# Loading w2 and the last query weights over two groups of a backward pass, and making rows in small tasks

## The chip, the cores and the metric

The kernel runs on one core of one Trainium2 chip. The metric is the device time of one execution in microseconds. The core has a matrix engine (PE), two engines for elementwise work (DVE and ACT), GpSimd (POOL) and SyncE (SP), and its transfers run on 16 DMA engines that SP, ACT and POOL issue to.

## The reference

A decoding step of one token is run through four layers, attention, MLP, attention, MLP, all with shared weights, and then everything is differentiated. One attention layer and one MLP layer:

```
q = layernorm(x) @ wq                      # 1024 -> 32 heads x 128
scores = q . k_cache * 128**-0.5           # 4 KV heads, 65536 positions
o = softmax(scores) . v_cache              # 8 query heads per KV head
x = x + o @ wo
h = relu(layernorm(x) @ w1 + b1) ** 2      # 1024 -> 3584
x = x + h @ w2 + b2
```

The outputs are the final x (out_0) and the gradients of x, k_cache, v_cache, wq, wo, w1, b1, w2 and b2. Everything is bfloat16. The two caches are 67 MB each and are read in every pass; their gradients are written, 67 MB each. The gradient of a weight is a sum of two outer products, one per layer that uses it.

## The kernel before, in words

There are four passes over K and V, each over four groups (the KV heads). A pass is a software pipeline of 256 items, 64 per group (`IPG`); an item is 8 blocks of 128 positions. The first two passes are the forward attention layers, the third (`attn_bwd3`) is the backward pass of the second attention layer, and the fourth (`attn_bwd4`) is that of the first and writes the gradients of K and V for both layers at once. A K or V slab of 1 MB holds 4 items.

**Third pass.** Item i transposes a V block group (`vT`, L799, copied out of PSUM at L152 or L155 by `evac`, which chooses ACT or DVE by a running count of their load), multiplies it (`vS`, L820) two items later, and uses K (`k8`, L842) eleven items after `vT`. `Stream.fetch` issues a slab on SP's queue (L249) at its first use in program order; SP runs ahead of the engines until the slot that it wants is free. The slots are a ring, least recently used first: areas 0 to 4 and 6 to 13 at the start of this pass, 13 slots of 1 MB. `ring.remove` takes a slot out.

**Background work.** `at(bg, i, fn)` hangs a task on item i. `in_order` ties the first instruction of a task on each engine behind the one before it there; otherwise the framework's scheduler orders instructions.

In the third pass the background does three things. `og3.later` makes dots of Wo rows for the next group. `qg3.early` makes dots of Wq rows with the finished groups' query gradients (`dot_va`, L380 on DVE and L381 on ACT): groups 0 and 1 together with eight loads of 512 KB through the ring, and group 2 with eight loads of 256 KB on ACT's queue (L749) into `area[5]`. And w2, needed twice: as it is for the forward MLP of layer 4 (`mv_slab`, L358, giving out_0), and transposed for the backward MLP of layer 2 (`pg2`, L1133). Its 28 blocks of 128 rows pass through a buffer of four rows in `area[6]`:

```
    i0 = IPG * (G - 1) + 10
    for k in range(8):
        at(bg, i0 - 14 + 8 * max(0, k - 1), lambda k=k: ring.remove(area[6 + k]))
    for kc in range(FC):
        at(bg, i0 + 2 * kc - 6, lambda kc=kc: w2_fetch(kc))
        at(bg, i0 + 2 * kc, lambda kc=kc: w2_block(kc))
    at(bg, i0 + 2 * FC, w2_done)
```

`w2_fetch` issues on SP's queue (L1099); `w2_block` multiplies, transposes (L1108) and copies the transposed block into areas 7 to 13. `w2_done` stores out_0 (L292, on SP's queue).

**Between the passes.** `qg3.last` loads the Wq columns of the last group after the pass and makes their dots by `row_dots` (L414 to L434), ending in L744. Then follow the layer norm's backward step, `pg2`, the dots of W1 (`RowDots`, with W1 loaded through the ring), another layer norm step, the first Wo dots and the start of the fourth pass. In the fourth pass the last group's Wq product is made another way: `qg1.transposed` has transposed the weights before, and `last_transposed` (L769 to L775) multiplies them with the column.

**Fourth pass.** Beside `vT`, `vS` and `k8` (with the K and V gradients made at L960 and stored at L967 and L968 by POOL's queue), a list of tasks (`gw_tasks`) is spread evenly over items 72 to 253. `rows_into` puts two columns into rows of `long_rows` or `short_rows` (casts at L976, products with the identity at L981 into `ps_gg`, copies on DVE at L982), up to 32 column blocks in one task; `outer2` makes pieces of the weight gradients (L1006) and stores them (L1010). `ps_gg` has two buffers, shared by the K and V gradients and all these tasks. `g_setup` prepares a group's operands (L867 to L885), at the first `vS` of the group.

Of the kernel before, what the change touches and what calls it, by code (L numbers as in the profile page):

```python
# [14 lines left out]
P = 128  # L15
# [3 lines left out]
def kernel(  # L19
# [830 lines left out]
    def attn_bwd4(La, Lb, oga, ogb, order, eTa, eTb, dqT, bg, group_done, streams):  # L850
# [4 lines left out]
        XT = Turn([blocks(small, i) for i in (3, 4)])  # L855
        XS = Turn([part(small, i, 1024) for i in (5, 6)])
        GGS = Turn([part(area[5], i, 512) for i in range(2)])
        ndt4 = part(small, 14, 512)[0:64, :].rearrange("p (s r) -> p s r", r=R2)
        ST = Turn([pair[6], pair[8], pair[10]])
        DOB = vec.tile([P, G, 4, R2], BF, name="DOB")  # L860
        nc.vector.memset(DOB[:], 0.0)
# [2 lines left out]

        def g_setup(g):
            sl = slice(g * R, (g + 1) * R)
            nc.vector.tensor_copy(out=DOB[:, g, 0, 0:R], in_=oga.dOT[:, sl])  # L867
            nc.vector.tensor_copy(out=DOB[:, g, 0, R:R2], in_=ogb.dOT[:, sl])
            CCf = tmp.tile([P, R4], F32, name="CCf")
            nc.vector.scalar_tensor_tensor(out=CCf[:, 0:R], in0=La["qT"][:, sl], scalar=SCALE, in1=La["rZ"][:, sl], op0=ALU.mult, op1=ALU.mult)  # L870
            nc.vector.scalar_tensor_tensor(out=CCf[:, R:R2], in0=Lb["qT"][:, sl], scalar=SCALE, in1=Lb["rZ"][:, sl], op0=ALU.mult, op1=ALU.mult)
            nc.vector.tensor_tensor(out=CCf[:, R2:3 * R], in0=oga.dOT[:, sl], in1=La["rZ"][:, sl], op=ALU.mult)
            nc.vector.tensor_tensor(out=CCf[:, 3 * R:R4], in0=ogb.dOT[:, sl], in1=Lb["rZ"][:, sl], op=ALU.mult)
            CC4 = tmp.tile([P, 4, R4], BF, name="CC4")
            nc.vector.tensor_copy(out=CC4[:, :, :], in_=CCf[:, :].unsqueeze(1).to_broadcast([P, 4, R4]))
            pt = ps_mv([P, P], BF)
            nc.tensor.transpose(pt[:, :], CC4[:].rearrange("p a b -> p (a b)"), ident_b[:, :])
            T4 = tmp.tile([P, P], F32, name="T4")
            nc.vector.tensor_copy(out=T4[:], in_=pt[:, :])
            GG = GGS.next().rearrange("p (c t d) -> p c t d", c=2, t=2)  # L880
            for c2 in range(2):
                for t in range(2):
                    nc.vector.tensor_scalar(out=GG[:, c2, t, :], in0=T4[:], scalar1=M4x[:, 2 * c2 + t:2 * c2 + t + 1], scalar2=None, op0=ALU.mult)
            nc.vector.tensor_copy(out=ndt4[:, :, 0:R], in_=oga.nd2[:, sl].unsqueeze(1).to_broadcast([64, UB4, R]))
            nc.vector.tensor_copy(out=ndt4[:, :, R:R2], in_=ogb.nd2[:, sl].unsqueeze(1).to_broadcast([64, UB4, R]))  # L885
            state[("G", g)] = GG
# [10 lines left out]

        def vS(idx):
            g, c8 = kit[idx]
            if c8 == 0:  # L900
                g_setup(g)
            vt = state.pop(("vt", idx))
            for i in range(8):
                c = c8 + i
                slot = c % UB4
                if slot == 0:
                    state["ps_dp"] = ps_sc([P, UB4, R2])
                    nc.tensor.matmul(state["ps_dp"][:, :, :].rearrange("p c r -> p (c r)"), lhsT=sel2[:, :],
                                     rhs=ndt4[:, :, :].rearrange("o c r -> o (c r)"), start=True, stop=False)
                ps_dp = state["ps_dp"]  # L910
                last = slot == UB4 - 1
                w = min(4, UB4 - slot)
                nc.tensor.matmul(ps_dp[:, slot:slot + w, :].rearrange("p a b -> p (a b)"), lhsT=vt[:, i, :],  # L913
                                 rhs=DOB[:, g, 0:w, :].rearrange("p a b -> p (a b)"), start=False, stop=last)
                if last:
                    c0 = c - slot
                    X = XS.next().rearrange("p (s r) -> p s r", r=R4)
                    ea = eTa[g][:, :, c0:c0 + UB4].rearrange("p h c -> p c h")
                    eb = eTb[g][:, :, c0:c0 + UB4].rearrange("p h c -> p c h")
                    nc.vector.tensor_tensor(out=X[:, :, 0:R], in0=ps_dp[:, :, 0:R], in1=ea, op=ALU.mult)  # L920
                    nc.vector.tensor_tensor(out=X[:, :, R:R2], in0=ps_dp[:, :, R:R2], in1=eb, op=ALU.mult)  # L921
                    nc.gpsimd.tensor_copy(out=X[:, :, R2:3 * R], in_=ea)
                    nc.gpsimd.tensor_copy(out=X[:, :, 3 * R:R4], in_=eb)
                    add_load(dve=2 * (0.07 + UB4 * R * 0.0021))
                    nblk = UB4 // 4
                    pt2 = ps_tr()
                    for bi in range(nblk):
                        nc.tensor.transpose(pt2[:, bi, :], X[:, 4 * bi:4 * bi + 4, :].rearrange("p a b -> p (a b)"), ident_b[:, :])  # L928
                    xt = XT.next()
                    evac(xt[:, 0:nblk, :], pt2[:, 0:nblk, :])  # L930
                    state[(g, c0 // UB4)] = (X, xt)

        def k8(idx):
# [32 lines left out]
            if j0 + 8 == J:  # L966
                nc.gpsimd.dma_start(out=GKv[g][b], in_=st[:, 0, :, :])  # L967
                nc.gpsimd.dma_start(out=GVv[g][b], in_=st[:, 1, :, :])  # L968

        pipeline(n, [(vT, 0), (vS, TLEAD), (k8, TLEAD + UB4 // 8 + 1)], bg)  # L970


    def rows_into(rows, cols, nj):
        cc = tmp.tile([P, 32, 2], BF, name="r2_cc")
        for l in range(2):
            nc.vector.tensor_copy(out=cc[:, 0:nj, l], in_=cols[l])  # L976
        for j0 in range(0, nj, 4):
            jn = min(4, nj - j0)
            pt = ps_gg()
            for jj in range(jn):  # L980
                nc.tensor.matmul(pt[0:2, jj * P:(jj + 1) * P], lhsT=cc[:, j0 + jj, :], rhs=ident_b[:, :], start=True, stop=True)  # L981
            nc.vector.tensor_copy(out=rows[0:2, j0 * P:(j0 + jn) * P], in_=pt[0:2, 0:jn * P])  # L982

    def outer2(stages, out_dram, a_rows, K, b_rows, c0, N):

# [101 lines left out]
    for j, g in enumerate(ORD3[1:]):  # L1087
        og3.later(vbc_small, g, bg, IPG * j + 12, 1)
    qg3 = QueryGrad(dqT3, "B3")
    qg3.early(ORD3[:2], bg, IPG * 2 + 14, 2.6, area[5])  # L1090
    qg3.early(ORD3[2:3], bg, IPG * 3 + 14, 3, area[5], Turn([part(area[5], i, 1024) for i in (1, 2, 3)]), 6)


    w2rows = Turn([part(area[6], i, 1024) for i in range(4)])
    w2T, w2_here = {}, {}

    def w2_fetch(kc):
        w2_here[kc] = w2rows.next()
        nc.sync.dma_start(out=w2_here[kc], in_=B_w2[kc * P:(kc + 1) * P, :])  # L1099

    def w2_block(kc):
        rows = w2_here.pop(kc)
        if kc == 0:
            L4["pf"] = ps_bg([P, DC])
        mv_slab(L4["pf"], rows, kc, FC, D, L4["gb"][:, kc:kc + 1])
        pt = ps_tr()
        for i in range(DC):
            nc.tensor.transpose(pt[:, i, :], part(rows, i, P), ident_b[:, :])  # L1108
        w2T[kc] = blocks(area[7 + kc // 4], kc % 4)
        evac(w2T[kc], pt[:, :, :])  # L1110

    def w2_done():
        mlp_close(L4, L4["pf"][:, :])
        col_to_dram(L4["xo"], D, out_0.rearrange("a b d -> (a b d)"))
    i0 = IPG * (G - 1) + 10
    for k in range(8):
        at(bg, i0 - 14 + 8 * max(0, k - 1), lambda k=k: ring.remove(area[6 + k]))
    for kc in range(FC):
        at(bg, i0 + 2 * kc - 6, lambda kc=kc: w2_fetch(kc))
        at(bg, i0 + 2 * kc, lambda kc=kc: w2_block(kc))  # L1120
    at(bg, i0 + 2 * FC, w2_done)
    attn_bwd3(L3, og3, ORD3, eT3, dqT3, bg)


    dn3 = qg3.last(ORD3[-1], area[5])
    dxn3 = ln_bwd(dn3[:], L3["n"], L3["rstd"])
    dx2 = add_cols(dx3[:], dxn3[:], "dx2")
    dx2b = tmp.tile([P, DC], BF, name="dx2b")
# [41 lines left out]
        nc.gpsimd.memset(long_rows, 0.0)  # L1170
        nc.gpsimd.memset(short_rows, 0.0)

    def rows_of(rows, cols, nj):
        return lambda: rows_into(rows, cols, nj)

    def gwq_tasks(gs, fresh=True):
        gs = sorted(gs)
        a, b = gs[0] * R, (gs[-1] + 1) * R
        if fresh:
            yield rows_of(short_rows, [L3["n"][:], L1["n"][:]], DC)  # L1180
        yield rows_of(long_rows, [dqT3[:, a:b], dqT1[:, a:b]], b - a)
        yield from outer2(stages, out_4, short_rows, D, long_rows, gs[0] * GD, len(gs) * GD)

    def gw_tasks():
        yield rows_of(short_rows, [gx[:], dx2[:]], DC)
        yield rows_of(long_rows, [L4["g"][:], L2["g"][:]], FC)
        yield from outer2(stages, out_8, long_rows, F, short_rows, 0, D)
        yield rows_of(short_rows, [L4["n"][:], L2["n"][:]], DC)
        yield rows_of(long_rows, [dh4[:], dh2[:]], FC)
        yield from outer2(stages, out_6, short_rows, D, long_rows, 0, F)  # L1190
        yield from gwq_tasks(ORD4[0:2])
        yield rows_of(short_rows, [dx3[:], dx1[:]], DC)
        yield rows_of(long_rows, [L3["oT"][:], L1["oT"][:]], HQ)
        yield from outer2(stages, out_5, long_rows, QD, short_rows, 0, D)
        yield from gwq_tasks(ORD4[2:3])

# [6 lines left out]
    qg1 = QueryGrad(dqT1, "B1")  # L1203
    done = [IPG * (j + 1) + LAG4 + 1 for j in range(G)]
    at(bg, done[0], rows_ready)
    i0, i1 = done[0] + 1, IPG * G - 3
    tasks = list(gw_tasks())
    for t, fn in enumerate(tasks):
        at(bg, i0 + t * (i1 - i0) // len(tasks), fn)
# [55 lines left out]
```

## Time and profile before

| | us |
|---|---|
| median of 3 runs | 2053.38 (2046.49 to 2057.97) |
| profiled execution | 2053.45 |
| span of its trace | 2051.7 |

| engine | busy us | share of the span |
|---|---|---|
| PE, matmuls | 1611.4 | 79% |
| PE, weight loads | 1325.5 | 65% |
| DVE | 1117.5 | 54% |
| ACT | 1025.1 | 50% |
| POOL | 187.6 | 9% |

Transfers: 802.26 MB, mean 391 GB/s; SP's queue carries 617.68 MB, POOL's 165.69 MB and ACT's 14.68 MB. The granted clock of PE is 0.891 in the mean.

In timelines each row has its start in us from the span's start, its length in us, engine, line, operation, output and inputs, and in brackets how long the engine sat idle before it and for what. "SPq", "ACTq" and "POOLq" are what an engine does as an issuer of transfers. In lists of waits each row says who waited for whom: us in total, number of times, the longest.

### The profile page before, as it was taken

To read this page: it belongs to the slowest core of one execution; us is meant where nothing else is said; L and a number is where in the kernel's file an instruction comes from. 1 tells how busy PE (TensorE), PEld (TensorE's weight loads), DVE (VectorE), ACT (ScalarE), POOL (GpSimd) and SP (SyncE) were. 2 spreads that over 40 slices of the span, in tenths; PEclk is the share of its full clock that TensorE was granted. 3 is DMA by queue.
4 is the path that set the end of the run, shared out by engine and by line. 5 is a ranking of instruction groups with operands and counts; after the bars stand their busy time and mean duration, and the time that the engine had idled before them with its cause. 6 is when DMAs were issued, how large, how long until landed. Compare 5 with 4: busy or idle time off the path is not lost. (4 is left out here: it accounts for less than half of the span.)

```text
span 2051.7 us, 65956 instructions
## 1 busy us (share of the span) xinstructions
PE 1611.4 (79%) x29812; PEld 1325.5 (65%) x29876; DVE 1117.5 (54%) x1814; ACT 1025.1 (50%) x1276; POOL 187.6 (9%) x334
## 2 busy tenths in 40 slices
PE   7888886588898846887788766887887868878786
PEld 7877776578887745777677765655555545545463
DVE  4543431255434304744463436877777758778685
ACT  4543432125443303434453335876675756757675
POOL 0000000000000000000000000222222212212122
PEclk9999997579999956899998876999999989989797
DMA  9999999999999996999998888799999999989996
GB/s 381 418 418 416 413 419 412 391 359 419 416 419 415 412 406 255 380 415 419 407 411 329 305 344 342 292 425 425 414 418 412 389 423 420 422 358 413 422 418 265
DMA packets 139869, 802.26 MB, mean 391 GB/s; under 512 B 14148, under 2 KB 14148, under 8 KB 58436
## 3 DMA queue, kind: packets, MB, share of 16 engines
q1 hardware_dynamic: 104676, 617.68, 74.1%
q0 software_dynamic: 26848, 165.69, 19.5%
q10 hardware_dynamic: 8064, 14.68, 1.9%
q8 instruction: 233, 3.82, 0.7%
q14 instruction: 48, 0.39, 0.0%
HBM read 632.30 MB, written 165.69 MB: 389 GB/s over the span
## 5 line engine op out<-in xcount | busy, mean ns | idle before, releaser
L155 DVE COPY small<-ps_tr 128x1024 bf16<-128x1024 bf16 x664 | 447.4, 686 | 361.3 <-PE ps_tr L555 172.1
L152 ACT COPY small<-ps_tr 128x1024 bf16<-128x1024 bf16 x376 | 377.1, 1015 | 408.9 <-PE ps_tr L555 231.3
L152 ACT CAST pair<-ps_gg 128x1024 bf16<-128x1024 f32 x292 | 293.5, 1017 | 140.0 <-PE ps_gg L960 99.0
L155 DVE CAST pair<-ps_gg 128x1024 bf16<-128x1024 f32 x220 | 268.3, 1221 | 114.6 <-PE ps_gg L960 79.6
L960 PE MATMUL ps_gg<-slot,small 64*128 64x512 bf16 x1024 | 202.0, 403 | 57.2 <-ACT pair L152 20.8
L574 PE MATMUL ps_sc<-L_qpad,small 128*128 128x64 bf16 (+7 forms) x3712 | 173.8, 193 | 25.9 <-ACT small L152 12.0
L555 PE MATMUL ps_tr<-ident_b,slot 128*128 128x128 bf16 x2304 | 163.4, 224 | 14.6 <-DMA slot<-in_A_k_cache_dram 13.2
L574 PEld LDWEIGHTS <-small 128*128 128x128 bf16 x3712 | 139.2, 99 | 44.3 <-ACT small L152 20.9
L617 PE MATMUL ps_acc<-eT,slot 128*128 128x64 bf16 x2720 | 130.4, 209 | 39.6 <-DMA slot<-in_A_v_cache_dram 37.6
L893 PE MATMUL ps_tr<-ident_b,slot 128*128 128x128 bf16 x1696 | 150.3, 225 | 12.4 <-DMA slot<-in_A_v_cache_dram 9.0
L555 PEld LDWEIGHTS <-slot 128*128 128x128 bf16 x2304 | 137.1, 100 | 17.5 <-DMA slot<-in_A_k_cache_dram 16.2
L617 PEld LDWEIGHTS <-slot 128*128 128x128 bf16 x2720 | 114.6, 107 | 44.0 <-DMA slot<-in_A_v_cache_dram 42.1
L893 PEld LDWEIGHTS <-slot 128*128 128x128 bf16 x1696 | 107.1, 100 | 53.8 <-issue 36.5
L960 PEld LDWEIGHTS <-small 64*128 64x128 bf16 x1024 | 59.9, 94 | 114.8 <-issue 86.6
L555 PE MATMUL ps_tr<-ident_b,pair 128*128 128x128 bf16 x1600 | 113.5, 223 | 12.4 <-DMA pair<-in_A_k_cache_dram 12.3
L913 PE MATMUL ps_sc<-DOB,small 128*128 128x64 bf16 (+3 forms) x2048 | 116.3, 195 | 1.2 <-issue 0.4
L820 PE MATMUL ps_sc<-B_dOpad,small 128*128 128x64 bf16 (+7 forms) x2048 | 100.6, 193 | 18.7 <-ACT small L152 9.1
L913 PEld LDWEIGHTS <-small 128*128 128x128 bf16 x2048 | 89.4, 100 | 38.5 <-issue 32.8
L381 ACT ACTIVATE pair<-pair 128x1024 bf16<-128x1024 bf16 (+1 forms) x80 | 92.2, 1153 | 30.2 <-DVE pair L380 27.8
L555 PEld LDWEIGHTS <-pair 128*128 128x128 bf16 x1600 | 94.7, 100 | 15.2 <-DMA pair<-in_A_k_cache_dram 14.2
L799 PE MATMUL ps_tr<-ident_b,slot 128*128 128x128 bf16 x1088 | 86.3, 234 | 21.5 <-DMA slot<-in_A_v_cache_dram 19.3
L580 DVE TENSOR_REDUCE pm_all<-pair 128x8 f32<-128x512 f32 x64 | 43.9, 686 | 108.6 <-ACT pair L579 108.5
(266 smaller groups left out, 2380.3 us busy)
## 6 DMA issues: line engine op xcount, KB each, us to landing
slot<-in_A_v_cache_dram SPq DMA_DIRECT2D x172, 1024.0 KB, 13.7
slot<-in_A_k_cache_dram SPq DMA_DIRECT2D x156, 1024.0 KB, 17.0
out_dram<-pair POOLq DMA_DIRECT2D x128, 1024.0 KB, 18.2
pair<-in_A_k_cache_dram SPq DMA_DIRECT2D x85, 1024.0 KB, 17.6
pair<-in_A_v_cache_dram SPq DMA_DIRECT2D x76, 1024.0 KB, 18.4
out_dram<-eT POOLq DMA_DIRECT2D x44, 512.0 KB, 18.4
slot<-in_A_wo_dram SPq DMA_DIRECT2D x16, 1024.0 KB, 14.5
pair<-in_B_w_dram SPq DMA_DIRECT2D x14, 896.0 KB, 16.1
```

Source lines behind the costliest of these rows:

```text
L152: nc.scalar.copy(out=out, in_=in_)
L155: nc.vector.tensor_copy(out=out, in_=in_)
L381: nc.scalar.activation(out=view, in_=view, func=ACTF.Copy, accum_out=ycol)
L555: nc.tensor.transpose(pt[:, i, :], kb8[:, i, :], ident_b[:, :])
L574: nc.tensor.matmul(ps_s[:, slot:slot + w, :].rearrange("p a b -> p (a b)"), lhsT=kt[:, i, :], rhs=L["qpad"][:, g, 0:w, :].rearrange("p a b ...
L580: nc.vector.tensor_reduce(out=pm_all[:, :, c0 // UB], in_=S_sb[:, :, c0:c0 + un], axis=AX.X, op=ALU.max)
L617: nc.tensor.matmul(ps_o[:, :, :].rearrange("p a b -> p (a b)"), lhsT=vb8[:, i, :], rhs=eT[g][:, :, c:c + 8], start=(c == 0), stop=(c == C ...
L799: nc.tensor.transpose(pt[:, i, :], vb8[:, i, :], ident_b[:, :])
L820: nc.tensor.matmul(ps_dp[:, slot:slot + w, :].rearrange("p a b -> p (a b)"), lhsT=vt[:, i, :], rhs=dOpad[:, g, 0:w, :].rearrange("p a b -> ...
L893: nc.tensor.transpose(pt[:, i, :], vb8[:, i, :], ident_b[:, :])
L913: nc.tensor.matmul(ps_dp[:, slot:slot + w, :].rearrange("p a b -> p (a b)"), lhsT=vt[:, i, :], rhs=DOB[:, g, 0:w, :].rearrange("p a b -> p ...
L960: nc.tensor.matmul(pg[:, t2 * 512:(t2 + 1) * 512], lhsT=xt[64 * t2:64 * t2 + 64, blk0 + half, :], rhs=GG[64 * t2:64 * t2 + 64, :, :, :].re ...
```

## The change

In the third pass w2 comes in seven loads of 1 MB, each straight into the area that keeps it, and each block is transposed in place; the last group's Wq comes the same way in two loads, into areas 6 and 5, and its product uses `last_transposed`. The ring gives up its slots one by one from item 84 to item 202; the loads start at items 100 (Wq), 116, 133 and so on to 218 (w2), and 234 (Wq). The Wq dots of groups 0 and 1 are made by rows on ACT's queue, as those of group 2 were. In the fourth pass `rows_into` is cut into tasks of four column blocks, whose copies `evac` gives to ACT or DVE, the task list ends at item 244 instead of 253, and the set-up of groups 1 to 3 is a background task three items ahead of the group's first, with two buffers for `ndt4`.

```diff
-        ndt4 = part(small, 14, 512)[0:64, :].rearrange("p (s r) -> p s r", r=R2)
+        NDT = Turn([part(small, i, 512)[0:64, :].rearrange("p (s r) -> p s r", r=R2) for i in (14, 15)])
...
-            if c8 == 0:
+            if idx == 0:
                 g_setup(g)
...
+        for j in range(1, G):
+            at(bg, IPG * j - 3, lambda j=j: g_setup(order[j]))
...
     def rows_into(rows, cols, nj):
-        cc = tmp.tile([P, 32, 2], BF, name="r2_cc")
-        for l in range(2):
-            nc.vector.tensor_copy(out=cc[:, 0:nj, l], in_=cols[l])
-        for j0 in range(0, nj, 4):
+
+        def piece(j0):
             jn = min(4, nj - j0)
+            cc = tmp.tile([P, 4, 2], BF, name="r2_cc")
+            for l in range(2):
+                nc.vector.tensor_copy(out=cc[:, 0:jn, l], in_=cols[l][:, j0:j0 + jn])
             pt = ps_gg()
             for jj in range(jn):
-                nc.tensor.matmul(pt[0:2, jj * P:(jj + 1) * P], lhsT=cc[:, j0 + jj, :], rhs=ident_b[:, :], start=True, stop=True)
-            nc.vector.tensor_copy(out=rows[0:2, j0 * P:(j0 + jn) * P], in_=pt[0:2, 0:jn * P])
+                nc.tensor.matmul(pt[0:2, jj * P:(jj + 1) * P], lhsT=cc[:, jj, :], rhs=ident_b[:, :], start=True, stop=True)
+            evac(rows[0:2, j0 * P:(j0 + jn) * P], pt[0:2, 0:jn * P], kind="f32")
+        for j0 in range(0, nj, 4):
+            yield lambda j0=j0: piece(j0)
...
-    qg3.early(ORD3[:2], bg, IPG * 2 + 14, 2.6, area[5])
-    qg3.early(ORD3[2:3], bg, IPG * 3 + 14, 3, area[5], Turn([part(area[5], i, 1024) for i in (1, 2, 3)]), 6)
+    wq_rows = Turn([part(area[5], i, 1024) for i in (1, 2, 3)])
+    for j in range(G - 1):
+        qg3.early(ORD3[j:j + 1], bg, IPG * (j + 1) + 14, 3, area[5], wq_rows, 6)
...
+    def in_place(ap, kc):
+        blk = blocks(ap, kc % 4)
+        pt = ps_tr()
+        for i in range(8):
+            nc.tensor.transpose(pt[:, i, :], blk[:, i, :], ident_b[:, :])
+        evac(blk, pt[:, :, :])
+        return blk
+
+    def take(ap, src, i, ahead, remove=True):
+        if remove:
+            at(bg, i - ahead, lambda: ring.remove(ap))
+        at(bg, i, lambda: nc.sync.dma_start(out=ap.rearrange("p (k n) -> p k n", n=1024), in_=src))
...
-    i0 = IPG * (G - 1) + 10
-    for k in range(8):
-        at(bg, i0 - 14 + 8 * max(0, k - 1), lambda k=k: ring.remove(area[6 + k]))
+    gl = ORD3[-1] * GD
+    i0 = IPG + 36
+    take(area[6], w_rows(A_wq, 0, 4, gl, GD), i0, 16)
+    for kc in range(4):
+        at(bg, i0 + 10 + 4 * kc, lambda kc=kc: wq_block(area[6], kc))
+    i0 += 16
+    for k in range(7):
+        take(area[7 + k], w_rows(B_w2, k * 512, 4, 0, D), i0 + 17 * k, 16)
     for kc in range(FC):
-        at(bg, i0 + 2 * kc - 6, lambda kc=kc: w2_fetch(kc))
-        at(bg, i0 + 2 * kc, lambda kc=kc: w2_block(kc))
-    at(bg, i0 + 2 * FC, w2_done)
+        at(bg, i0 + 10 + int(4.25 * kc), lambda kc=kc: w2_block(kc))
+    at(bg, i0 + 10 + 17 * 7, w2_done)
+    i0 = IPG * (G - 1) + 42
+    take(area[5], w_rows(A_wq, 512, 4, gl, GD), i0, 0, False)
+    for kc in range(4, 8):
+        at(bg, i0 + 8 + 3 * (kc - 4), lambda kc=kc: wq_block(area[5], kc))
...
-    dn3 = qg3.last(ORD3[-1], area[5])
+    qg3.wT = wqT
+    dn3 = qg3.last_transposed(ORD3[-1])
...
-            yield rows_of(short_rows, [L3["n"][:], L1["n"][:]], DC)
-        yield rows_of(long_rows, [dqT3[:, a:b], dqT1[:, a:b]], b - a)
+            yield from rows_into(short_rows, [L3["n"][:], L1["n"][:]], DC)
+        yield from rows_into(long_rows, [dqT3[:, a:b], dqT1[:, a:b]], b - a)
...
-    i0, i1 = done[0] + 1, IPG * G - 3
+    i0, i1 = done[0] + 1, IPG * G - 12
```

More of the change, by code (lines that the diff above doesn't have):

```diff
@@ L866, in g_setup @@
             sl = slice(g * R, (g + 1) * R)
+            ndt4 = state[("ndt", g)] = NDT.next()
             nc.vector.tensor_copy(out=DOB[:, g, 0, 0:R], in_=oga.dOT[:, sl])
@@ L908, in vS @@
                     nc.tensor.matmul(state["ps_dp"][:, :, :].rearrange("p c r -> p (c r)"), lhsT=sel2[:, :],
-                                     rhs=ndt4[:, :, :].rearrange("o c r -> o (c r)"), start=True, stop=False)
+                                     rhs=state[("ndt", g)][:, :, :].rearrange("o c r -> o (c r)"), start=True, stop=False)
                 ps_dp = state["ps_dp"]
@@ L1089, with wq_block @@
     qg3 = QueryGrad(dqT3, "B3")
-    qg3.early(ORD3[:2], bg, IPG * 2 + 14, 2.6, area[5])
-    qg3.early(ORD3[2:3], bg, IPG * 3 + 14, 3, area[5], Turn([part(area[5], i, 1024) for i in (1, 2, 3)]), 6)
[L1094 to L1099, printed above, removed]
+    wq_rows = Turn([part(area[5], i, 1024) for i in (1, 2, 3)])
[12 more added lines that the diff above has]
+        at(bg, i, lambda: nc.sync.dma_start(out=ap.rearrange("p (k n) -> p k n", n=1024), in_=src))
+    w2T, wqT = {}, {}
     def w2_block(kc):
-        rows = w2_here.pop(kc)
+        ap = area[7 + kc // 4]
         if kc == 0:
             L4["pf"] = ps_bg([P, DC])
[L1105 to L1110, printed above, removed]
+        mv_slab(L4["pf"], part(ap, kc % 4, D), kc, FC, D, L4["gb"][:, kc:kc + 1])
+        w2T[kc] = in_place(ap, kc)
+    def wq_block(ap, kc):
+        wqT[kc] = in_place(ap, kc)
     def w2_done():
@@ L1171, in rows_ready @@
         nc.gpsimd.memset(short_rows, 0.0)
-    def rows_of(rows, cols, nj):
-        return lambda: rows_into(rows, cols, nj)
     def gwq_tasks(gs, fresh=True):
@@ L1179, in gwq_tasks @@
         if fresh:
-            yield rows_of(short_rows, [L3["n"][:], L1["n"][:]], DC)
-        yield rows_of(long_rows, [dqT3[:, a:b], dqT1[:, a:b]], b - a)
+            yield from rows_into(short_rows, [L3["n"][:], L1["n"][:]], DC)
+        yield from rows_into(long_rows, [dqT3[:, a:b], dqT1[:, a:b]], b - a)
         yield from outer2(stages, out_4, short_rows, D, long_rows, gs[0] * GD, len(gs) * GD)
     def gw_tasks():
-        yield rows_of(short_rows, [gx[:], dx2[:]], DC)
-        yield rows_of(long_rows, [L4["g"][:], L2["g"][:]], FC)
+        yield from rows_into(short_rows, [gx[:], dx2[:]], DC)
+        yield from rows_into(long_rows, [L4["g"][:], L2["g"][:]], FC)
         yield from outer2(stages, out_8, long_rows, F, short_rows, 0, D)
-        yield rows_of(short_rows, [L4["n"][:], L2["n"][:]], DC)
-        yield rows_of(long_rows, [dh4[:], dh2[:]], FC)
+        yield from rows_into(short_rows, [L4["n"][:], L2["n"][:]], DC)
+        yield from rows_into(long_rows, [dh4[:], dh2[:]], FC)
         yield from outer2(stages, out_6, short_rows, D, long_rows, 0, F)
         yield from gwq_tasks(ORD4[0:2])
-        yield rows_of(short_rows, [dx3[:], dx1[:]], DC)
-        yield rows_of(long_rows, [L3["oT"][:], L1["oT"][:]], HQ)
+        yield from rows_into(short_rows, [dx3[:], dx1[:]], DC)
+        yield from rows_into(long_rows, [L3["oT"][:], L1["oT"][:]], HQ)
         yield from outer2(stages, out_5, long_rows, QD, short_rows, 0, D)
```

## The prediction, made before the changed kernel was run

> **What bounds the kernel now.** I read the page's slices first, then the busy time by stage, then what SP's DMA queue waited for, then the order of time at three places. The page moves 802.26 MB, and the slices that run full carry 415 to 425 GB/s, so the kernel is bound by transfers wherever something keeps the queues filled, and time is lost where nothing does. By stage (span us, length, busy us per engine, granted clock, DMA share, GB/s):
>
> ```profile
> 850.00:1090.00 240.00, 194.87 (x4365) 176.34 (x4364) 122.27 (x202) 109.17 (x145) 0.00 (x0) 0.97 1.01 414
> 1090.00:1213.00 123.00, 93.37 (x1908) 88.05 (x1906) 47.99 (x72) 46.50 (x55) 0.00 (x0) 0.88 0.84 313
> 1213.00:1283.00 70.00, 42.00 (x725) 37.50 (x722) 41.91 (x109) 33.97 (x45) 3.28 (x5) 0.66 0.87 343
> 1283.00:2000.00 717.00, 588.49 (x7762) 387.66 (x7824) 538.18 (x728) 503.67 (x570) 171.61 (x297) 0.92 0.98 404
> ```
>
> The first row is most of the third pass: transfers are full. The second is its last group, where w2 is fetched: transfers run at three quarters, and no engine does better than PE's 93.37 of 123 us. The third is the serial stretch between the passes. Why is the second row starved? Waits of SP's queue from 1090 to 1215 (total us, times, longest):
>
> ```profile
> SPq L1099 <- PE ps_tr L1108: 85.8, 24, 11.2
> SPq L292 <- DVE ctd_rows L291: 9.5, 1, 9.5
> SPq L249 <- PE ps_acc L842: 0.9, 1, 0.9
> ```
>
> L1099 is the fetch of a w2 row block, L249 the fetch of K and V. SP issues in order; a w2 fetch waits until PE has transposed the block four before it, and the next K or V slab stands behind it. So K and V are issued about two steps ahead of use, as SP's own order of time shows:
>
> ```profile
> 1084.52 0.33 SPq L249 DMA_DIRECT2D slot<-in_A_v_cache_dram  x1
> 1098.90 0.33 SPq L1099 DMA_DIRECT2D pair<-in_B_w_dram  x1
> 1099.28 0.42 SPq L249 DMA_DIRECT2D slot<-in_A_k_cache_dram  x1
> 1102.54 0.33 SPq L1099 DMA_DIRECT2D pair<-in_B_w_dram  x1
> ```
>
> Nothing is issued for 14 us, and from then on one slab per w2 block.
>
> **Term 1: w2 in 1 MB loads over two groups.** The 28 fetches of 256 KB and their row buffer go; seven of 1 MB come, each into a slot taken out of the ring 16 items earlier. The slabs in that slot are consumed within 4 items of their issue, so SP's wait at such a load is for PE some 12 items back, not 2. Bytes do not change, PE's 448 w2 matmuls neither (163 ns and 219 ns each in the rows, pipelined), nor the 28 evictions (1.01 us on ACT or 0.69 on DVE); they spread over 130 items instead of 56. The second row moved 313 x 123 = 38.5 MB, which at the 417 GB/s of the full slices takes 92.3 us: 30.7 us less. Moving the last Wq (2.1 MB) in costs 5.0 us, so 25.7 us. PE must hold the pace: the first stage did 18.2 matmuls per us and kept transfers full; all matmuls of both stages with 64 more transposes are 6337 in 240 + 97 us, 18.8 per us. 1230 to 1240 us shows 24 per us, so this fits with a fifth to spare. From this I take off 3 us: from item 202 on the ring has five slots, SP is then about six items (8 us) ahead, and landing took 5.5 to 8.4 us in that stage, so the margin is thin. **23 us**, between 0 and 28: the low end is the ring starving transfers as the queue did. A loss below nothing is the rival below.
>
> Added waits. The load into area[5] (item 234) waits for ACT's last Wq dot at item 228, six items back, what the ring allows anyway. The store of out_0 moves from the end into item 245, with the last slabs behind it: SP waited 9.5 us there in the row above, with only Wq behind; in the new order K and V up to item 248 are ahead of it, so I cost it at nothing, covered by the slabs that are already in flight; without that cover up to 7 us.
>
> Wq dots of groups 0 and 1 leave SP's queue (eight loads of 512 KB) and go by rows on ACT's, 16 more issues. ACT's row for such an issue is 0.34 us, so 5.4 us of ACT, which is 45% busy in that stage: nothing. Their lead is 6 items, 8 to 9 us; landing there took 5.3 us in a thin stage, but 9.4 us in the full fourth pass (median). Where late, DVE and ACT stall in order and evictions with them: at most 16 x 1 us, and the ring of ten slots or more hides it then; up to 5 us, in the low end. The Trainium skill, "DMA: Bandwidth & Descriptors", section "Issuing engines are not separate DMA queues", says that a second issuing engine saves only the time to initiate; by it this part gains nothing, which speaks against making it. Its section "Anatomy of one DMA" gives about 2.0 us fixed plus bytes at 436 GB/s; if the fixed parts were exposed, 28 loads becoming 7 would save an estimated 42 us by that page, instead of the 30.7 us of the rows.
>
> **Term 2: the last Wq product.** Today it is a chain after the pass: load, multiply or transpose, copy, dot. Its ends, and the same work by transposed weights as the fourth pass already does it:
>
> ```profile
> 1214.97 0.17 DVE L845 SCALAR_TENSOR_TENSOR B_dqT<-ps_acc,L_rZ 128x8 f32<-128x8 f32 x1 [1.84 <-PE ps_acc L842]
> 1226.81 0.18 DVE L744 COPY B_dny<-B_dnl 128x8 f32<-128x8 f32 x1
> ...
> 2022.28 0.17 DVE L769 CAST dq_b<-B_dqT 128x8 bf16<-128x8 f32 x1
> 2022.55 1.67 PEld L773 LDWEIGHTS <-eT 128*128 128x128 bf16 x64 [0.23 <-issue]
> 2024.34 0.17 DVE L775 COPY B_dny<-ps_sc 128x8 f32<-128x8 f32 x1 [0.46 <-PE ps_sc L773]
> ```
>
> From 1215.14 to 1226.99 is 11.85 us; from 2022.28 to 2024.51 is 2.23 us. The difference is 9.6 us; at the lower clock of this stretch (0.5 to 0.84) the 64 matmuls may take 1 us more, so **9 us**, all on the path: layer norm, pg2, the W1 dots and the fourth pass follow one another. What is late next is W1: it is needed 13 us after (1240 against 1227), and its first five slabs are now issued as the ring's slots come free, earlier than today, when out_0 and Wq stand ahead. Bounds 5 to 10.
>
> **Term 3: the fourth pass.** Rows are made in pieces of four columns as single tasks. The largest of today's tasks sits in the deepest hole of this pass; DVE and POOL around it:
>
> ```profile
> 1826.15 5.17 DVE L982 CAST pair<-ps_gg 2x512 bf16<-2x512 f32 x8
> 1842.51 0.53 POOL L967 DMA_DIRECT2D out_dram<-pair  x1 [20.45 <-DVE pair L155]
> ```
>
> and the rates of the two deepest stretches (columns as in the first fence):
>
> ```profile
> 1580.00:1620.00 40.00, 35.68 (x453) 22.85 (x455) 30.82 (x44) 26.79 (x29) 8.91 (x16) 0.93 0.94 364
> 1830.00:1860.00 30.00, 27.90 (x339) 18.23 (x342) 23.47 (x35) 21.11 (x24) 5.79 (x10) 0.87 0.77 296
> ```
>
> Eight 2x512 copies in a row hold the two ps_gg buffers; no store is issued for 20 us and the rate falls. At 423 GB/s the two rows lose 5.6 and 9.0 us, and 1470 to 1500 (399 GB/s) 1.7 more, each after such a task: 16 us. Spread out, the copies remain (40 of 0.67 us, part on ACT now); 28 more casts of each kind at 0.16 us are 9 us of DVE in 450, and a wait of PE for a cast (2.4 us at the longest today) can come 38 times instead of 10. I take half, **8 us**, between -5 and 16. The group set-up five steps earlier has its small ops on DVE off the boundary, where the rates are full today (1798 us: 423): nothing. Tasks end nine items earlier; their stores (about 1.6 MB, 4 us) go from the thin tail into a full stage: nothing either way.
>
> **Sum.** The profiled execution took 2053.45 us (span 2051.7), as the median of the runs, 2053.38. 2053.45 - 23 - 9 - 8 = 2013.45, say 2013 us. A difference of 0.5% (10 us) is about what a measurement can tell from no change.
>
> **Rivals.**
> (a) The ring is what binds, mildly: transfers in the second group and the last improve only by half. For it: landing of 5.5 to 8.4 us against about 8 us of lead. 12 us instead of 23, and 4 of 8 in the fourth pass: 2053 - 12 - 9 - 4 = 2028, up to 2043 with the pieces costing more.
> (b) Slower: ring depth. The ring shrinks from item 84 on, not from 188. If transfers fall to 313 GB/s as soon as nine slots are left (item 134), 77.6 MB go at 313 instead of 417: 61.8 us, less the 30.7 lost today, +31; less 9 and 8: 2067. It breaks even if the low rate begins at seven slots. For it: the low rate was seen with a shrinking ring. Against: at 1084 us SP stopped on PE L1108, not on a slot (0.9 us for L249), with nine or ten slots still there, and the first two passes run at 416 with ten.
> (c) No net change: term 1 near nothing and the fourth pass pays back term 2 (38 pieces x 0.4 us): about 2052.
>
> **How the numbers follow.** Forecast (2000 to 2029) 0.66; (a) 0.20; (c) 0.06; (b) 0.08. All of the first two are faster by over 10 us: 0.86. The range takes 2013 with its bounds and (a): 1998 to 2043. Below 1998 would need 28 + 10 + 16.
>
> **What would show it.** Right: no 14 us gap of SP near 1085; 405 GB/s or more until the last K slab; the last B_dqT of the third pass near 1192 instead of 1215, B_dny 2 to 3 us after it; pg2 near 1195; no stretch of ten us under 350 GB/s between 1300 and 1980 (counted from this profile, 33 us earlier). Wrong: waits of SP on L249 for PE of tens of us after item 130; DVE or ACT waiting for in_A_wq rows in groups 1 and 2; PE waiting for r_cc casts by more than 20 us in the fourth pass.

## The result, and the profile after

The changed kernel takes 2034.68 us in the median of five runs (2031.86 to 2036.77), the kernel before 2052.51 beside it on the same chip (2046.49 to 2057.97): a ratio of 0.9914, with a 95% interval of 0.9891 to 0.9936. It is faster by 18 us where 40 were forecast. The profiled execution after took 2034.68 us (span 2032.9), so it stands for the median.

The span is cut at three events that both traces have: the last B_dqT of the third pass, the first B_dqT of the fourth pass and its last one (us).

| | last B_dqT, third pass | from it to the first, fourth pass | first to last, fourth pass | from there to the end |
|---|---|---|---|---|
| before | 1215.0 | 216.6 | 590.5 | 29.6 |
| after | 1208.1 | 207.0 | 591.2 | 26.6 |
| gain | 6.9 | 9.6 | -0.7 | 3.0 |
| forecast | 23 (Term 1) | 9 (Term 2) | 8 (Term 3), with the next column | |

Term 2 came as forecast, Term 1 brought less than a third, Term 3 hardly anything. The stages, with the columns of the prediction's first fence (the second row is shorter than before, as the stage is):

```profile
850.00:1090.00 240.00, 195.84 (x4320) 179.17 (x4320) 124.11 (x207) 111.26 (x146) 0.00 (x0) 0.95 0.99 400
1090.00:1206.00 116.00, 93.05 (x2025) 85.95 (x2024) 50.06 (x75) 47.23 (x56) 0.00 (x0) 0.94 0.96 385
1265.00:1981.00 716.00, 581.69 (x7768) 382.39 (x7824) 530.64 (x762) 514.67 (x592) 174.12 (x299) 0.95 0.99 403
```

The second row is what the change was to mend: 313 GB/s before, 385 now. But the first row, which was full (414), is now at 400: the change made a new hole in a stage that had none. Narrower stretches, same columns, show where:

```profile
900.00:930.00 30.00, 25.25 (x510) 22.36 (x507) 15.88 (x25) 13.89 (x19) 0.00 (x0) 0.89 1.02 411
930.00:960.00 30.00, 20.75 (x415) 18.87 (x414) 16.79 (x34) 15.61 (x24) 0.00 (x0) 0.88 0.81 302
960.00:1090.00 130.00, 106.31 (x2354) 97.51 (x2351) 64.53 (x105) 61.25 (x80) 0.00 (x0) 0.96 1.02 413
...
1160.00:1170.00 10.00, 8.09 (x180) 7.33 (x177) 5.61 (x8) 4.90 (x6) 0.00 (x0) 1.00 0.75 287
...
1180.00:1190.00 10.00, 8.45 (x198) 7.80 (x195) 4.23 (x8) 3.95 (x4) 0.00 (x0) 1.00 0.76 312
1190.00:1200.00 10.00, 9.18 (x215) 8.64 (x213) 5.51 (x8) 4.96 (x5) 0.00 (x0) 1.00 0.89 344
```

At 413 GB/s the stretch from 930 to 960 loses 8 us, the ones after 1160 another 7. What SP's queue waited for, first from 850 to 1090, then from 1090 to 1210 (us in total, times, longest; the head of each list and the two loads that matter here):

```profile
SPq L249 <- DMA slot<-in_A_wq_dram: 55.5, 9, 13.5
SPq L249 <- PE ps_acc L842: 38.0, 15, 4.5
```

```profile
SPq L249 <- PE ps_tr L799: 36.5, 16, 4.9
...
SPq L1112 <- ACT slot L381: 9.9, 1, 9.9
SPq L292 <- DVE ctd_rows L291: 8.4, 1, 8.4
```

The short waits for PE are the ordinary pace of the ring. The first line is all but new (0.9 us in the kernel before, from 850 to 1070): L249 is a K or V load, and it waits for the landing of a Wq row, with which it shares neither data nor buffer. Order of time of SP's issues, then of ACT's:

```profile
921.02 0.33 SPq L249 DMA_DIRECT2D pair<-in_A_k_cache_dram  x1
934.89 0.33 SPq L249 DMA_DIRECT2D pair<-in_A_v_cache_dram  x1
```

```profile
927.63 0.34 ACTq L749 DMA_DIRECT2D slot<-in_A_wq_dram  x1
934.36 0.34 ACTq L749 DMA_DIRECT2D slot<-in_A_wq_dram  x1
```

SP issues nothing for 14 us. The trace's records of the transfers, which name the completion counter of each, tell why: SP's 606 transfers and ACT's 72 share eight counters, GpSimd's 190 have eight of their own, and one that takes a counter waits until the transfer that held it has landed. SP's load of 934.89 takes the counter of ACT's load of 927.63; its load of 938.07 takes that of ACT's load of 934.36, which landed at 938.00. An ACT transfer is issued only when ACT comes to it in its own order; until then the SP load eight places behind it cannot go, nor any load after that.

The end of the third pass answers to the prediction's rows under Term 2:

```profile
1208.06 0.17 DVE L845 SCALAR_TENSOR_TENSOR B_dqT<-ps_acc,L_rZ 128x8 f32<-128x8 f32 x1 [4.62 <-PE ps_acc L842]
...
1210.37 0.17 DVE L775 COPY B_dny<-ps_mv 128x8 f32<-128x8 f32 x1 [1.94 <-PE ps_mv L773]
```

2.31 us from B_dqT to B_dny, where it was 11.85.

### The profile page after: what moved, and what is told of

Read it like the earlier page. It is cut to its first block, busy times and chain, and to the rows that moved or that the text cites. A ratio compares the mean times of both kernels' runs of the same rounds, so it can differ in the third digit from the quotient of the medians.

```text
span 2032.9 us, 66059 instructions
## 1 busy us (share of the span) xinstructions
PE 1595.6 (78%) x29876; PEld 1314.8 (65%) x29932; DVE 1107.4 (54%) x1842; ACT 1031.6 (51%) x1292; POOL 188.5 (9%) x334
## 5 line engine op out<-in xcount | busy, mean ns | idle before, releaser
L152 ACT COPY small<-ps_tr 128x1024 bf16<-128x1024 bf16 x381 | 382.2, 1015 | 419.5 <-PE ps_tr L555 232.8
L152 ACT CAST pair<-ps_gg 128x1024 bf16<-128x1024 f32 (+1 forms) x315 | 304.6, 982 | 126.9 <-PE ps_gg L961 80.1
L155 DVE CAST pair<-ps_gg 128x1024 bf16<-128x1024 f32 (+1 forms) x237 | 280.1, 1182 | 108.6 <-PE ps_gg L961 82.3
L555 PE MATMUL ps_tr<-ident_b,slot 128*128 128x128 bf16 x2304 | 163.5, 224 | 15.1 <-DMA slot<-in_A_k_cache_dram 12.8
L894 PE MATMUL ps_tr<-ident_b,slot 128*128 128x128 bf16 x1696 | 153.2, 227 | 20.5 <-DMA slot<-in_A_v_cache_dram 17.6
L574 PEld LDWEIGHTS <-small 128*128 128x128 bf16 x3712 | 138.4, 98 | 44.7 <-ACT small L152 20.9
L914 PE MATMUL ps_sc<-DOB,small 128*128 128x64 bf16 (+3 forms) x2048 | 110.9, 193 | 0.5
L914 PEld LDWEIGHTS <-small 128*128 128x128 bf16 x2048 | 85.8, 99 | 36.2 <-issue 31.6
L799 PE MATMUL ps_tr<-ident_b,slot 128*128 128x128 bf16 x1248 | 93.7, 228 | 12.2 <-DMA slot<-in_A_v_cache_dram 9.4
L820 PEld LDWEIGHTS <-small 128*128 128x128 bf16 x2048 | 80.8, 100 | 31.0 <-ACT small L152 15.6
```

The source lines that it names most:

```text
L152: nc.scalar.copy(out=out, in_=in_)
L155: nc.vector.tensor_copy(out=out, in_=in_)
L555: nc.tensor.transpose(pt[:, i, :], kb8[:, i, :], ident_b[:, :])
L574: nc.tensor.matmul(ps_s[:, slot:slot + w, :].rearrange("p a b -> p (a b)"), lhsT=kt[:, i, :], rhs=L["qpad"][:, g, 0:w, :].rearrange("p a b ...
L799: nc.tensor.transpose(pt[:, i, :], vb8[:, i, :], ident_b[:, :])
L894: nc.tensor.transpose(pt[:, i, :], vb8[:, i, :], ident_b[:, :])
```

## Experiments: the missing 16 us of Term 1

**Theory 1:** the Wq rows on ACT's queue hold SP back, 8 us, and two added waits of SP (L1112, L292) cost most of the rest. **Theory 2:** the ring, smaller from item 84 on, is what binds. Unless said otherwise an edit is made to the changed kernel. The runs were made in sets, with medians of the kernel before from 2052.51 to 2055.24 us, so kernels of different sets are compared by their ratios.

**Wq rows issued by GpSimd.**

```diff
-        def __init__(self, dqT, lname):
+        def __init__(self, dqT, lname, queue=None):
+            self.queue = queue or nc.scalar
-            nc.scalar.dma_start(out=box[kc][:, 0, :], in_=A_wq[...])
+            self.queue.dma_start(out=box[kc][:, 0, :], in_=A_wq[...])
-    qg3 = QueryGrad(dqT3, "B3")
+    qg3 = QueryGrad(dqT3, "B3", nc.gpsimd)
```

> The changed kernel with one edit: in the third pass the 24 loads of Wq rows are issued by POOL instead of ACT; same bytes, same buffers, same items. Theory 1 (shared completion counters): SP's and ACT's transfers take eight completion counters in turn, so a K or V load on SP's queue waits until the Wq load that had its counter before has landed, and that one is issued only when ACT gets there in its order. Then SP's waits for in_A_wq (32.7 + 22.8 + 2.8 us in the changed kernel) go to nothing, the hole of 8.3 us at 930 to 960 us goes, and the time falls by 6 to 10 us, to about 2026. Rival theory 2 (the Wq rows themselves: small pieces, or DVE and ACT stalled in order for rows that land late): the hole stays wherever the loads are issued, and the time is within 3 us of 2034.7.

Measured: 2026.99 us, ratio 0.9871 (0.9853 to 0.9889), some 8 us less than the changed kernel (0.0043 of 2053 is 8.8, the medians differ by 7.7). The last B_dqT of the third pass comes at 1199.8 instead of 1208.1, 8.3 us earlier; the later columns of the table move by less than 4 us each. SP's waits for in_A_wq are gone, and the hole with them:

```profile
930.00:960.00 30.00, 22.00 (x456) 20.11 (x453) 18.05 (x34) 16.01 (x27) 3.22 (x6) 0.89 1.02 412
```

Same loads, same buffers, same ring; another issuing engine with other counters. That is Theory 1 for these 8 us.

**The Wq load into area[5] and the out_0 store off SP as well** (on top of the last one).

```diff
-        nc.sync.dma_start(out=v1d.rearrange(...), in_=rows[:])
+        (queue or nc.sync).dma_start(out=v1d.rearrange(...), in_=rows[:])
-        col_to_dram(L4["xo"], D, out_0.rearrange(...))
+        col_to_dram(L4["xo"], D, out_0.rearrange(...), nc.gpsimd)
-    take(area[5], w_rows(A_wq, 512, 4, gl, GD), i0, 0, False)
+    take(area[5], w_rows(A_wq, 512, 4, gl, GD), i0, 0, False, nc.gpsimd)
```

> As e1, and two more transfers are taken off SP's queue in the third pass: the second Wq load (into area 5) and the store of out_0 are issued by POOL. Theory 1 with in-order stalls: SP's waits of 9.9 us (for ACT) and 8.4 us (for DVE) in the last group go, the rate at 1160 to 1200 us (287, 312 and 344 GB/s) rises to 400 or more, and another 5 to 9 us go: about 2019, with the last B_dqT of the third pass near 1192. Rival (five slots are too few in the last group, whatever stands in the queue): no more than 3 us under e1.

Measured: 2022.88 us, ratio 0.9849 (0.983 to 0.9869); last B_dqT at 1194.0, 5.8 us earlier again. By the medians it is 4.1 us faster than the run before, between the 5 to 9 of Theory 1 and the 3 of the rival, and the two intervals overlap; the rate settles it for Theory 1, with 410 to 419 GB/s from 1160 to 1190 where 287 and 312 were. The stage row, and what GpSimd's queue waited for from 850 to 1200:

```profile
1090.00:1192.00 102.00, 84.80 (x1912) 78.39 (x1912) 47.72 (x71) 45.41 (x54) 3.96 (x7) 0.97 1.00 399
```

```profile
POOL out_dram L292 <- DVE ctd_rows L291: 20.4, 1, 20.4
POOL slot L1113 <- ACT slot L381: 19.5, 1, 19.5
```

The waits are not shorter, they are longer; they only stand where no K or V load is queued behind them. B_dqT is now 2 us from the 1192 of the prediction, so the 16 us that Term 1 missed are 8.3 (ACT's queue), 5.8 (two waits of SP) and 2 that remain; the ring may be those, at 399 instead of 417 GB/s.

**Wq of groups 0 and 1 by the ring, as before the change.**

```diff
-    for j in range(G - 1):
-        qg3.early(ORD3[j:j + 1], bg, IPG * (j + 1) + 14, 3, area[5], wq_rows, 6)
+    qg3.early(ORD3[:2], bg, IPG * 2 + 14, 2.6, area[5])
+    qg3.early(ORD3[2:3], bg, IPG * 3 + 14, 3, area[5], wq_rows, 6)
```

> The changed kernel with the Wq dots of groups 0 and 1 as they were: both together in the third group, eight loads of 512 KB through the ring on SP's queue; only group 2's rows come on ACT's queue. Theory 1 and theory 2 both say that the hole at 930 to 960 us goes (no such load there any more) and the time falls by 5 to 10 us, to about 2027, less what the second group's bytes cost later; against e1 it tells whether moving the loads at all was worth anything: theory 1 says e4 and e1 are within 4 us of each other, theory 2 says that e4 is faster than e1 by 5 us or more.

Measured: 2032.39 us, ratio 0.9906 (0.9891 to 0.992): 5 us from what both theories gave, and 5.4 us slower than the first run, where Theory 1 had the two within 4 us and Theory 2 had this one faster. From 930 to 960 the rate is 415 GB/s, so the old hole is gone, but a new one opens, with a wait of SP from 850 to 1210 behind it:

```profile
1020.00:1060.00 40.00, 31.31 (x645) 29.23 (x646) 27.44 (x52) 23.17 (x37) 0.00 (x0) 0.87 0.89 337
```

```profile
SPq L249 <- ACT slot L381: 36.2, 9, 7.1
```

Slots that hold Wq come free only when ACT has made the dots (L381), and the ring now shrinks in the same stretch. So the rows were worth taking off the ring, if they are issued by GpSimd; it was the queue that was ill chosen.

**A longer lead for the Wq rows on ACT's queue.**

```diff
-        qg3.early(ORD3[j:j + 1], bg, IPG * (j + 1) + 14, 3, area[5], wq_rows, 6)
+        qg3.early(ORD3[j:j + 1], bg, IPG * (j + 1) + 14, 3, area[5], wq_rows, 9)
```

> The changed kernel with the Wq rows of the third pass still on ACT's queue, but issued nine items ahead of their dot instead of six. If SP stands because a load on ACT's queue holds the counter that SP's next load needs, then issuing that load three items (about 4 us) earlier shortens each long wait of SP by about as much: 32.7 us of waits for in_A_wq at 850 to 1000 us fall to 20 or less, and the time falls by 3 to 6 us, to about 2030. If the wait were for bandwidth or for the dots, an earlier issue changes nothing (2032 to 2037).

Measured: 2035.78 us, ratio 0.9906 (0.9887 to 0.9924): nothing gained, a miss. From 850 to 1210 SP now waits more, not less:

```profile
SPq L249 <- DMA slot<-in_A_wq_dram: 91.8, 14, 15.3
```

But the nine items were not had. There are three row buffers and a dot every three items, so a lead of nine uses them up: in this trace the fourth, fifth and sixth load of the second group are issued at 930.27, 938.32 and 943.53 us, each within 0.03 us of the end of the ACT dot (L381) that frees the buffer, 2 to 4 us earlier than in the changed kernel (934.36, 940.57, 945.76), and the seventh and eighth at the old times. So this run says little of a longer lead; why SP's waits grew is open.

**The kernel before, with w2's loads issued by GpSimd.** One word changes; layout, ring, Wq and rows stay as they were. (The text on record counts eight transposing loads; these are the 28 plain ones of 256 KB.)

```diff
-        nc.sync.dma_start(out=w2_here[kc], in_=B_w2[kc * P:(kc + 1) * P, :])
+        nc.gpsimd.dma_start(out=w2_here[kc], in_=B_w2[kc * P:(kc + 1) * P, :])
```

> The kernel before, with one edit: the eight transposing loads of w2 are issued by GpSimd's queue in place of SP's; everything else, Wq products and rows included, is as before. Theory 1 (what the change frees is SP's queue: the gap of 14 us near 1085 and the ones around it exist because SP stands at w2's loads): the K and V loads no longer stand behind those of w2, the last B_dqT of the third pass comes some 18 to 23 us earlier than the 1215 us of the kernel before (1192 to 1197), and the time falls by as much, a ratio of 0.989 to 0.991. Theory 2 (the slab ring is what holds SP there, so that SP waits for slots whoever issues w2): the last B_dqT moves by less than 5 us, ratio above 0.9975.

Measured: 2025.53 us, ratio 0.9864 (0.9848 to 0.9881), 28 us faster than the kernel before and 9 to 10 faster than the changed one (medians, ratios). That is more than the 18 to 23 us that were expected. The last B_dqT comes at 1190.0. The stage of w2 and the waits of GpSimd's queue from 1065 to 1230:

```profile
1090.00:1188.00 98.00, 85.16 (x1957) 80.25 (x1953) 47.93 (x72) 46.56 (x55) 12.89 (x24) 0.97 0.99 398
```

```profile
POOL pair L1099 <- PE ps_tr L1108: 82.0, 22, 21.0
```

82.0 us of waits for PE, as SP had 85.8 before, and 398 GB/s instead of 313. So the reading of the old profile was right: the queue, not the size of the loads and not the ring, held K and V back. Its size too: 38.5 MB, which took 123 us, take 97 at 398 GB/s, 26 us less, and B_dqT came 25.0 earlier. SP stood 22.0 us in this stage for rows of Wq that ACT issues (four waits, 9.9 at the longest), and still the stage ran at 398 GB/s: a total of waits is not yet a price. Of the rest, 3 us are in the tail (26.6 us), which this edit does not touch: a tail moves by that much without its own tasks being changed.

## Experiments: Term 3

**The fourth pass as before the change.** Set-up at the boundary, rows in one task on DVE, the list ending at item 253.

```diff
-            ndt4 = state[("ndt", g)] = NDT.next()
-        for j in range(1, G):
-            at(bg, IPG * j - 3, lambda j=j: g_setup(order[j]))
-            yield from rows_into(...)
+            yield rows_of(...)
-    i0, i1 = done[0] + 1, IPG * G - 12
+    i0, i1 = done[0] + 1, IPG * G - 3
```

> The changed kernel with its fourth-pass part undone (rows in one task each, all their copies on DVE, group set-up at the group's first item, tasks until item 253). If the two traces are right that the fourth pass gained about 2 us in all, it takes 2037 (2033 to 2041). If the prediction's 8 us were real and hidden by something else, 2042 or more. If the small tasks cost more than they save, less than 2032, and the holes of the old kernel at 1583 to 1620 and 1830 to 1860 come back but those at 1694 to 1724 and 1784 to 1834 go.

Measured: 2037.28 us, ratio 0.9922 (0.9906 to 0.9938). The interval overlaps that of the changed kernel: Term 3 is worth some 2 us, not told from nothing, and what the trace shows of it lies in the tail (29.5 against 26.6 us).

**Rows in one task, the rest as after.**

```diff
+        yield lambda: rows_once(rows, cols, nj)   # the body of before
-        for j0 in range(0, nj, 4):
-            yield lambda j0=j0: piece(j0)
```

> The changed kernel with rows made in one task per call again, all their copies on DVE; the early group set-up and the list's end at item 244 stay. With e6 and the undone fourth pass it splits that part in three. If small tasks are worth nothing (holes only spread), 2033 to 2037, with deep short holes in place of the shallow long ones; if they are worth the prediction's 8 us, 2040 or more; theory 3 says the former.

Measured: 2037.96 us, ratio 0.9914 (0.9898 to 0.9931), that of the changed kernel. Splitting the rows is worth nothing that these runs could tell; an interval reaches some 3 us to each side.

**The list ending at item 253.**

```diff
-    i0, i1 = done[0] + 1, IPG * G - 12
+    i0, i1 = done[0] + 1, IPG * G - 3
```

> The changed kernel with its task list ending at item 253 again, as before. The traces say that the stretch from the last B_dqT of the fourth pass to the end of the span is 29.6 us before and 26.6 after; if the earlier end of the list does that, 3 us come back: about 2038, tail near 29.5. The prediction costed this at nothing: 2035.

Measured: 2040.17 us, ratio 0.9928 (0.9911 to 0.9945), a tail of 29.4 us. It has the sign that was expected, inside the interval's width. But the run before this one, whose list ends at item 244, has a tail of 29.2 us as well, so the end of the list alone does not set the tail.

**No rows at all.** The tasks that make the rows do nothing, so the weight gradients come from rows of zeros.

```diff
-            yield lambda j0=j0: piece(j0)
+            yield lambda j0=j0: None
```

> The changed kernel with the rows of the fourth pass left out (the tasks of rows_into are there, each does nothing, so the four weight gradients are made of rows that stay zero; pacing, outer products and stores are the same). It bounds what any way of making the rows can save. Theory 3 (the rows' work is the cost, however it is cut: casts, products and copies by engines that are already at three quarters, while no store of a weight gradient keeps the queues full): the holes at 1694 to 1724 and 1784 to 1834 us go and the time falls by 8 to 16 us, to about 2023. Rival 4 (the holes have nothing to do with rows, they come from pacing or from the outer products): within 3 us of 2034.7, holes where they were.

Measured: 2029.35 us, ratio 0.9879 (0.9861 to 0.9897), 7 us less than the changed kernel by the ratios (5 by the medians; by the intervals anything from 1 to 13): all that any way of making rows can bring there, under the low end that was expected. The fourth pass from its first to its last B_dqT, after and with no rows (columns as before):

```profile
1416.00:2006.60 590.60, 479.64 (x6127) 311.50 (x6179) 432.13 (x629) 417.59 (x484) 143.25 (x247) 0.93 1.00 407
```

```profile
1416.00:2004.00 588.00, 465.58 (x5975) 305.48 (x6036) 420.67 (x531) 408.96 (x466) 142.12 (x247) 0.92 1.00 409
```

11 us of DVE and 9 of ACT go, and the pass is 3 us shorter. It runs at 407 or 409 GB/s whatever the rows do. Of three holes of the changed kernel two go with the rows (1701 to 1721 is at 418 GB/s, 1781 to 1801 at 424; 364 and 365 with rows a us earlier), the third stays (1801 to 1821 at 373, 367 with rows).

**Fewer pieces**, on top of the kernel with the Wq rows, the area[5] load and the out_0 store on GpSimd: eight columns a piece, through bf16 transposes.

```diff
-            jn = min(4, nj - j0)
+            jn = min(8, nj - j0)
-            pt = ps_gg()
+            pt = ps_gg()[:, :].bitcast(BF)
-                nc.tensor.matmul(pt[0:2, ...], lhsT=cc[:, jj, :], rhs=ident_b[:, :], start=True, stop=True)
-            evac(rows[0:2, ...], pt[0:2, 0:jn * P], kind="f32")
+                nc.tensor.transpose(pt[0:2, ...], cc[:, jj, :], ident_b[:, :])
+            evac(rows[0:2, ...], pt[0:2, 0:jn * P])
```

> As e2_three_off_sp, with the rows of the fourth pass made in pieces of eight columns through bf16 transposes, so half as many tasks and evictions of half the bytes. If what the rows still cost is the work of their pieces (leaving all rows out gave back some 7 us, of which half would be the pieces), the time falls by 2 to 4 us against e2_three_off_sp, a ratio of 0.983. If the fourth pass goes at the rate that its loads allow whatever the pieces cost, it stays at the ratio of e2_three_off_sp, 0.985, within 0.002.

Measured: 2017.04 us, ratio 0.9825 (0.981 to 0.984), 6 us below the kernel that it builds on by the medians, 5 by the ratios. The ratio is the 0.983 that was expected for gains by the pieces' work; the intervals of the two just overlap (0.983 to 0.984). It is the fastest kernel of this study. Copies of the rows in the changed kernel, then in this one (busy us, mean ns, idle before):

```profile
L152 ACT CAST pair<-ps_gg 2x512 bf16<-2x512 f32 x23 | 13.2, 573 | 20.0 <-PE ps_gg L985 19.9
L155 DVE CAST pair<-ps_gg 2x512 bf16<-2x512 f32 x17 | 11.4, 673 | 4.0 <-PE ps_gg L985 3.9
```

```profile
L152 ACT COPY pair<-ps_gg 2x1024 bf16<-2x1024 bf16 x10 | 10.0, 1000 | 11.0 <-PE ps_gg L986 11.0
L155 DVE COPY pair<-ps_gg 2x1024 bf16<-2x1024 bf16 x9 | 6.1, 678 | 3.9 <-PE ps_gg L986 3.7
```

DVE copies 1024 bf16 in the time of 512 f32 (678 ns, 673), and 40 copies become 21 (two more of 512 are left out here). The pass is 588.6 us from first to last B_dqT, 6.5 less than in the kernel that it builds on (595.1), but much the same as 587.9 in the run without rows. As the kernels' passes vary from 587.9 to 595.1 us, how much of these 5 to 6 us is the pieces' work and how much the way in which tasks fall on items stays open.

## Why the prediction was right and wrong

**What bounds (right).** SP's order of issue starved the second stage. Moving only w2's loads to another queue brings it from 313 to 398 GB/s and B_dqT from 1215.0 to 1190.0. Rivals (a) and (b), in which the ring binds, fall with it: with the ring as small as in the changed kernel and the Wq rows, the area[5] load and the out_0 store on GpSimd, the stage from 850 to 1090 ran at 414 GB/s and the next one at 399.

**Term 1 (23 us, came to 7).** The gain itself was sized well: without the three costs below, B_dqT came 21 us earlier. These costs were put at nothing, and they were 14 us. PE did hold the pace (1912 matmuls in 102 us, at 399 GB/s), but the stretch that showed a fifth to spare, 1230 to 1240, was no measure of it: 213 of its 243 matmuls have one column.
- *Wq rows on ACT's queue: "nothing", worst 16 x 1 us by stalls of DVE and ACT.* Those stalls were there (6.7 and 6.0 us), but the step failed elsewhere: it looked at ACT's time and at the readers of the rows, and not at SP, which stood 55.5 us at loads for landings of these rows. Cost: some 8 us (the first run with GpSimd). The prediction quoted the rule of the Trainium skill, "DMA: Bandwidth & Descriptors", section "Issuing engines are not separate DMA queues", that a second issuing engine saves only initiation. The runs go further on both sides. ACT's issues cost 8 us, through the counters that they share with SP's. GpSimd's, for w2, saved 28, because an engine that waits before it issues also holds back what it would issue next.
- *The area[5] load, "what the ring allows anyway".* SP stood 9.9 us for ACT's dot, since SP runs ahead of the items and came to this load at 1153 us, 10 us before the dot six items back had been made.
- *The out_0 store, covered by slabs in flight.* SP stood 8.4 us, much as the 9.5 before, and the rate fell to 312 and 344 GB/s: the cover was not there. Both waits together cost 5.8 us, under the 7 that the prediction named for the store without its cover.

**Term 2 (9 us, 9.6 came).** Right in size and place: 2.31 us after B_dqT, and the first B_dqT of the fourth pass, 207 us on, has kept the gain. In the run that only moves w2's loads, and so keeps the old product, that stretch still takes 215.7 us.

**Term 3 (8 us, some 2).** The step that failed is "half of 16 us of holes". It took the hole of 1830 to 1860 for the price of the task that lay in it. With the rows split there are other holes, and the first two of these go when the rows are left out:

```profile
1700.00:1720.00 20.00, 17.41 (x262) 11.73 (x263) 15.42 (x28) 15.79 (x20) 5.01 (x10) 1.00 0.97 364
...
1780.00:1800.00 20.00, 15.20 (x179) 9.10 (x180) 15.04 (x25) 12.82 (x17) 3.85 (x7) 0.82 0.95 365
1800.00:1820.00 20.00, 16.07 (x231) 10.28 (x232) 17.07 (x39) 13.25 (x19) 3.45 (x6) 0.91 0.92 367
```

These three lose 8 us at 423 GB/s, and the forecast sign failed: 1700 to 1710 goes at 347 and 1810 to 1820 at 315, where no ten us under 350 were to be left. The whole pass moves 407 GB/s, as before (0.98 DMA share in the prediction's fourth row, 0.99 now). The runs bound the term: one task or pieces make no difference, no rows at all 7 us. What keeps that pass from 423 GB/s was not found.

**Sum.** The kernel with those three transfers on GpSimd, at 2022.88, is where 2053.45 - 23 - 9 = 2021 would be. That is partly chance: at the first B_dqT of the fourth pass it is 29.9 us ahead of the kernel before, then it loses 4.6 us in that pass and gains 5.1 in the tail, and the prediction has a reason for neither. The measured 2034.68 lies where rival (a) put it (2028, up to 2043), but not by its mechanism, a ring that binds.

## What to carry to other kernels

When a queue that issues in order is the bound, ask of every transfer left on it or put beside it what that transfer will wait for, and what is queued behind; a load whose wait can be long belongs on an engine that issues nothing urgent, and that is worth trying before a new layout: w2's loads on GpSimd's queue, one changed word, gave 28 us, the whole change 18. A hole in the transfers beside a large task is no price for the task; leave the task's work out in one run and see what there is to gain before cutting it in pieces.

## What the runs showed of the hardware

Loads issued by SP and by ACT were not independent here: SP stood up to 13.5 us for an ACT transfer to land, and 55.5 us in all, with no data and no buffer in common, because both take the same eight completion counters in this build. GpSimd's transfers have eight others: with the same rows issued there, SP had no such wait. The stage with w2 in 256 KB loads issued by GpSimd ran at 398 GB/s, the same stage with loads of 1 MB at 399, and at 405 in the fastest kernel; but w2 is at most 7.3 of the 39 MB of that stage, and most of the rest is K and V. The prediction's 42 us come from the fixed 2.0 us per transfer of the Trainium skill, "DMA: Bandwidth & Descriptors", section "Anatomy of one DMA", which the page gives for loads issued by GpSimd, while SP issued those of the kernel before; nothing of that size showed even in the run where GpSimd issued them.
